# One constant 128x512 product in front of the turns of q, P, x, the sealed rows and the logits, in an attention plus top-2 expert kernel

## The chip, the cores and the metric

The kernel runs on one core of a Trainium2 chip. The core has a matrix engine (TensorE, PE in the profile; its weight loads are shown as PEld), a vector engine (VectorE, DVE), a scalar engine (ScalarE, ACT), GpSimd (POOL) and SyncE (SP), which run their own instruction streams and meet at semaphores. Sixteen DMA engines move data between HBM and the on-chip memory SBUF. TensorE writes only to PSUM, which has eight banks of 128 partitions by 512 float32; the vector and scalar engines read it from there. The metric is the device time of one launch in microseconds (us); a median of several runs is compared.

## The reference

The work is a chunked attention followed by a mixture of experts. There are 4 batches, 8 heads, 768 positions and a head size of 64. Chunks of 32 queries see 16 keys before them, their own 32, 8 after them, and 8 memory keys, 64 in all. The output is 3072 rows of 512 numbers, and each row goes to 2 of 8 experts.

```python
for c in range(nc):                        # 24 chunks of 32 queries
    k_full = np.concatenate([mem_k, k_ctx], axis=2)
    v_full = np.concatenate([mem_v, v_ctx], axis=2)
    scores = scale * np.matmul(q_c, k_full.transpose(0, 1, 3, 2))
    a = np.exp(scores - np.max(scores, axis=-1, keepdims=True))
    out[:, :, c_start:c_end] = np.matmul(a / np.sum(a, -1, keepdims=True), v_full)
x = out.transpose(0, 2, 1, 3).reshape(3072, 512)
noisy_logits = x @ w_gate + np.log1p(np.exp(x @ w_noise)) * noise
top2, top2_w = two largest of noisy_logits, softmax over the two
for e in range(8):                          # F = 1024
    h = np.maximum(x[mask] @ w1[e], 0.0)
    out[mask] += top2_w[mask, k, None] * (h @ w2[e])
```

## The kernel before

**Attention.** Heads are taken in 16 pairs (4 per batch); two pairs form a group, and q, k and v are loaded by group. For every pair q and k are turned on TensorE (`turn`, line 505: 12 transposes of 128x64 each into a PSUM buffer of class Q) and copied to SBUF by ScalarE or VectorE. `scores` (line 529) writes the 24 chunks of one pair to PSUM; VectorE takes the maximum (line 546) and subtracts it (line 562), ScalarE takes the exponential (line 565). The probabilities P are turned by `pt` (line 568: 6 transposes of 128x128 into a PSUM buffer of class G), copied (lines 355 and 357), and multiplied with the values in `pv` (line 581: 6 products with the memory values, line 584, and 24 with the windows, line 587). VectorE divides (line 605) into the rows x. After the second pair of a group `xtp` (line 610) turns x for both pairs, 6 transposes each into a G buffer, and the copies feed `logits` (line 647: 24 products of 16 columns, one G buffer per batch).

**Routing.** Per batch, a chain of small VectorE operations and products (lines 662 to 867: `sel`, `rank`, `place`, `table`, `spare_rank`) finds for each pair of experts the list of its rows; the rows of x go to HBM (line 871). There are 28 pairs of experts with a tile of 128 places each.

**Experts.** Rows are gathered by indirect DMA from POOL (line 907), turned by `xturn` (line 932: 4 transposes per tile), multiplied with w1 (`ups`, line 977, products at line 1013), passed through a relu (line 1023), multiplied with w2 (`downs`, products at line 1054), weighted and added on VectorE, and scattered to the output by POOL (line 1085). For the first two experts half of each tile (the sealed half, `half == 0`) is gathered from the first three batches alone, so that its turns (four of them) and its w1 products lie beside the routing of the last batch.

**Order.** A planner (`Planner`, line 60) simulates the engines with the cost written at each `op` and emits every operation in the order of its start; that order is the order of each engine's instruction stream. An engine takes its instructions in that order, and a waiting one holds up those behind it. The buffers of a class go round: class Q has two PSUM banks, class G two during the attention and six more after it, and a new holder waits until the readers of the former one are done. The q, k, v and weight loads and the gathers are issued by POOL and share its DMA queue; the rows of x are written from SP.

`turn`, `pt`, `xtp` and `xturn` each run their transposes back to back with the moving operand `identb`, the 128x128 identity.

Of the kernel before, what the change touches and what calls it, by code (L numbers as in the profile page):

```python
# [12 lines left out]
F32 = mybir.dt.float32  # L13
# [182 lines left out]
def kernel(  # L196
# [117 lines left out]
    identb = const.tile([128, 128], BF16, name="identb")  # L314
# [36 lines left out]
    V, A, P_, G_ = nc.vector, nc.scalar, nc.tensor, nc.gpsimd  # L351
# [7 lines left out]
    op, buf = pl.op, pl.buf  # L359
    DA = lambda d, a: [("DVE", d), ("ACT", a)]  # L360

    def ident_fn(o):
        make_identity(nc, identb)

# [96 lines left out]
    for g in range(NG):  # L461
        b, gg = divmod(g, 2)
        bq, bk, bv = buf("q"), buf("k"), buf("v")
# [32 lines left out]
    for n in range(NPAIR):  # L496
        g, j = divmod(n, 2)
        b, i = divmod(n, PB)
        bq, bk, bv, lq, lk, lv = groups[g]
# [2 lines left out]
        if i == 0:  # L502
            xrows[b] = buf("xrow")

        def turn(o, src, dst, j=j):
            s = src.t.rearrange("p h (t d) -> p h t d", t=TP)
            for t in range(TP):
                for hh in range(2):
                    P_.transpose(out=dst.t[64 * hh:64 * hh + 64, t * QP:(t + 1) * QP], in_=s[:, j + 2 * hh, t, :], identity=identb)  # L509
# [51 lines left out]
        else:  # L561
            sb = op("sb", ("DVE", 0.98), lambda o, bmx=bmx, bS=bS, bsd=bsd: V.tensor_tensor(  # L562
                out=bsd.t, in0=sv(bS), in1=bmx.t.rearrange("p x (u o) -> p x u o", o=1).to_broadcast([128, 2, BT, CTX]), op=Alu.subtract),
                deps=[mx], alloc=[bsd], use=[bS, bmx], prio=pr - 3, tag="attn")
            ex = op("ex", ("ACT", 0.85), lambda o, bsd=bsd, bP=bP: A.activation(out=bP.t.rearrange("p (x u) h c -> p x (u h) c", x=2), in_=bsd.t, func=Act.Exp, scale=scale), deps=[sb], alloc=[bP], use=[bsd], prio=pr - 2, tag="attn")  # L565
        gP, bPT = buf("G"), buf("PT")

        def pt(o, gP=gP, bP=bP):
            d = gP.t.bitcast(BF16)[:, :BT * 128].rearrange("p (u q) -> p u q", q=128)
            for u in range(BT):  # L570
                P_.transpose(out=d[:, u, :], in_=bP.t[:, u, :, :], identity=identb)
# [36 lines left out]
        gX, bxt = buf("G"), buf("xt")  # L608

        def xtp(o, gX=gX, b=b, i=i):  # L610
            d = gX.t.bitcast(BF16)[:, :BT * 128].rearrange("p (u q) -> p u q", q=128)
            x4 = xrows[b].t.bitcast(BF16)
            for u in range(BT):
                P_.transpose(out=d[:, u, :], in_=x4[:, u, 128 * i:128 * (i + 1)], identity=identb)  # L614
# [11 lines left out]
    for b in range(B):  # L626
# [4 lines left out]
        gL = buf("G")  # L631
# [12 lines left out]
        def lv_(gL=gL):  # L644
            return gL.t[:, :BT * 2 * E].rearrange("p (t e) -> p t e", e=2 * E)

        def logits(o, b=b, lv_=lv_):
            l = lv_()
            for t in range(BT):
                for i in range(PB):  # L650
                    P_.matmul(out=l[:, t, :], lhsT=pairs[b * PB + i]["bxt"].t[:, t, :], rhs=wgn[:, i, :], start=(t == 0 and i == 0), stop=(i == PB - 1), skip_group_check=True)
# [275 lines left out]
    def turn_ops(units, prio, half):  # L927

        gx = buf("G", QM if half == 0 else None)
        m = len(units)  # L930

        def xturn(o):
            d = gx.t.bitcast(BF16)[:, :KP * m * 128].rearrange("p (j k c) -> p j k c", k=KP, j=m)
            for j, (ps, (bx, g)) in enumerate(units):
                s_ = bx.t.bitcast(BF16)
                n = SL if half == 0 and len(ps) == 1 else 128
                for kp in range(KP):
                    P_.transpose(out=d[:, j, kp, :n], in_=s_[:n, kp * 128:(kp + 1) * 128], identity=identb[:n, :n])

        tt = op("tt_a" if half == 0 else "tt", ("PE", 0.27 * m), xturn, deps=[u[1][1] for u in units] + [c_ident], alloc=[gx], use=[u[1][0] for u in units], prio=prio)  # L940
        if half is None:
            i0 = place_of(*units[0][0][0])

            def xev(o):
                copy(o.eng, XS[:, :, i0:i0 + m].rearrange("p k j c -> p j k c"), gx.t.bitcast(BF16)[:, :KP * m * 128].rearrange("p (j k c) -> p j k c", k=KP, j=m))

            w = KP * m * 128
            ev = op("xev", DA(0.2 + w / 1900, 0.2 + w / 1250), xev, deps=[tt], use=[gx], prio=prio)
            for ps, _ in units:
                turned_ev[ps[0], 0] = turned_ev[ps[0], 1] = ev  # L950
            return
        for j, (ps, _) in enumerate(units):
            def xev(o, j=j, ps=ps):
                d = gx.t.bitcast(BF16)[:, 512 * j:512 * j + 512].rearrange("p (k c) -> p k c", k=KP)
                i = place_of(*ps[0])
                if len(ps) == 1:
                    copy(o.eng, XS[:, :, i, SL * half:SL * half + SL], d[:, :, SL * half:SL * half + SL])
                elif half == 0:
                    copy(o.eng, halves_view(XS[:, :, i:i + 2], 0), d.rearrange("p k (x c) -> p k x c", x=2))
                else:  # L960
                    copy(o.eng, XS[:, :, i, SL:], d[:, :, SL:])
                    copy(o.eng, XS[:, :, i + 1, :SL], d[:, :, :SL])

            w = KP * (64 if len(ps) == 1 else 128)
            d_ = 0.4 if half and len(ps) > 1 else 0.2
            ev = op("xev_a" if half == 0 else "xev", ("ACT", 0.2 + w / 1250) if half == 0 else DA(d_ + w / 1900, d_ + w / 1250), xev, deps=[tt], use=[gx], prio=prio)
            for p in ps:
                turned_ev[p, half] = ev
# [256 lines left out]
```

## Time and profile before

| | before |
|---|---|
| median of 3 runs | 334.55 us (332.03 to 334.84) |
| the profiled execution's own time | 331.19 us |
| its span, first to last instruction | 329.6 us |
| TensorE busy | 282.8 us (86%), 3090 products |
| VectorE busy | 161.9 us (49%) |
| ScalarE busy | 141.0 us (43%) |
| GpSimd busy | 127.4 us (39%) |
| mean granted TensorE clock | 0.936 |

The page of the profile shows the span in 40 slices of 8.24 us. The row PEclk is the share of full speed that was granted to TensorE; the trace records it in stretches that are multiples of 3.41 us, each at full or at half speed. A wait's releaser is what ended an engine's idle time; "issue" there means that nothing in the profile was waited for.

### The profile page before, as it was taken

The numbers are of one execution on the slowest core, as the hardware profiler recorded it, in microseconds if no ns is written. First come the engines' busy times: TensorE is split into PE (matmuls) and PEld (weight loads), VectorE is DVE, ScalarE is ACT, GpSimd is POOL, SyncE is SP. The second block draws the span as 40 slices with busy tenths as digits, with TensorE's granted clock in tenths as the row PEclk, the third lists the DMA queues.
The fourth block names the chain that finished last, engine by engine and source line by source line (L and its number), as shares of the span: only waits on it lengthen the run. The fifth ranks groups of instructions, "written<-read, shape, count | busy, mean of one in ns | idle before, by whom it ended". The sixth has DMA issues, their size and how long they took to land.

```text
span 329.6 us, 7497 instructions
## 1 busy us (share of the span) xinstructions
PE 282.8 (86%) x3090; PEld 178.0 (54%) x3090; DVE 161.9 (49%) x404; ACT 141.0 (43%) x265; POOL 127.4 (39%) x148
## 2 busy tenths in 40 slices
PE   1678767587676799799999999999999999999991
PEld 0567655475566567455647645444544744744540
DVE  6877997879889676254253043052042051041050
ACT  1468665656484265741504604604604604505500
POOL 8293353413504915898735221041040051051072
PEclk9999797979785569999999999999999999999997
DMA  9999999999993592939999995395390020021032
GB/s 99 202 157 148 180 148 176 193 133 204 145 166 114 152 153 59 182 98 195 191 215 220 255 196 74 55 207 74 57 203 28 3 113 23 2 111 50 3 121 83
DMA packets 83065, 42.75 MB, mean 130 GB/s; under 512 B 57017, under 2 KB 76474, under 8 KB 83026
## 3 DMA queue, kind: packets, MB, share of 16 engines
q0 software_dynamic: 74672, 38.78, 87.3%
q1 hardware_dynamic: 8066, 3.38, 4.2%
q8 instruction: 25, 0.41, 0.5%
q14 instruction: 14, 0.11, 0.2%
q10 hardware_dynamic: 288, 0.07, 0.1%
HBM read 61.26 MB, written 10.85 MB: 219 GB/s over the span
## 4 chain that ended last, share of the span: by engine, by line
PE 50%; DMA 12%; POOL 12%; issue 11%; DVE 10%; ACT 2%; POOLq 1%; DVEq 0%
PE ps_l L1013 16%; PE ps_l L1054 15%; DMA vg<-in_v_dram 9%; PE ps_g L1054 6%; PE ps_g L1013 5%; POOL xl L907 4%; DMA w2l<-in_moe_w_dram 3%; POOL out_dram L1085 2%; POOL rest L910 2%; POOL vg L479 2%; DVE vg L368 2%; DVE xrow L605 2%; PE ps_o L587 1%; PE ps_g L614 1%; ACT kT L355 1%
## 5 line engine op out<-in xcount | busy, mean ns | idle before, releaser
L1023 ACT ACTIVATE ht<-ps_l 128x384 bf16<-128x384 f32 (+2 forms) x123 | 54.8, 470 | 94.5 <-PE ps_l L1013 93.0
L1054 PEld LDWEIGHTS <-ht 128*128 128x128 bf16 x448 | 43.7, 98 | 52.2 <-DMA w2l<-in_moe_w_dram 0.6
L1013 PE MATMUL ps_l<-XS,w1t 128*128 128x384 bf16 (+4 forms) x416 | 61.0, 302 | 2.8 <-ACT XS L355 2.8
L1013 PEld LDWEIGHTS <-w1t 128*128 128x128 bf16 x544 | 43.9, 99 | 33.4 <-issue 4.3
L1085 POOL DMA_INDIRECT out_dram<-acc,oid x28 | 28.8, 1027 | 70.2 <-DVE acc L1073 66.4
L1054 PE MATMUL ps_l<-w2l,ht 128*128 128x512 bf16 x240 | 53.4, 379 | 0.3 <-DMA w2l<-in_moe_w_dram 0.3
L479 POOL DMA_DIRECT2D vg<-in_v_dram x18 | 23.6, 1314 | 34.7 <-PE ps_o L587 30.6
L1073 DVE SCALAR_TENSOR_TENSOR acc<-ps_l,gates,acc 128x512 f32<-128x512 f32 x17 | 12.8, 751 | 45.6 <-PE ps_l L1054 43.6
L1073 DVE SCALAR_TENSOR_TENSOR acc<-ps_g,gates,acc 128x512 f32<-128x512 f32 x11 | 8.3, 751 | 37.4 <-PE ps_g L1054 37.4
L355 ACT COPY kT<-ps_q 64x768 bf16<-64x768 bf16 x27 | 21.4, 792 | 11.7 <-PE ps_q L509 10.2
L1065 DVE TENSOR_SCALAR acc<-ps_l,gates 128x512 f32<-128x512 f32 x20 | 15.0, 751 | 19.0 <-PE ps_l L1054 18.8
L1054 PE MATMUL ps_g<-w2l,ht 128*128 128x512 bf16 x96 | 21.7, 379 | 0.0
L907 POOL DMA_INDIRECT xl<-x_rows,gid x16 | 16.8, 1049 | 11.6 <-PE ps_l L1054 4.0
L1013 PEld LDWEIGHTS <-w1l 128*128 128x128 bf16 x192 | 17.2, 98 | 7.0
L1013 PE MATMUL ps_l<-XS,w1l 128*128 128x256 bf16 (+3 forms) x152 | 20.5, 289 | 0.0
L509 PE MATMUL ps_q<-identb,qn 128*64 128x128 bf16 x192 | 10.7, 256 | 10.8 <-DMA qn<-in_q_dram 7.3
L1023 ACT ACTIVATE ht<-ps_g 128x384 bf16<-128x384 f32 (+2 forms) x37 | 16.8, 479 | 6.7 <-PE ps_g L1013 5.8
L1013 PE MATMUL ps_g<-XS,w1t 128*128 128x384 bf16 (+4 forms) x128 | 19.6, 300 | 0.0
L919 DVE COPY gates<-xl 64x8 f32<-64x8 f32 (+1 forms) x40 | 11.5, 291 | 14.4 <-DMA xl<-x_rows,gid_b 8.3
L1054 PE MATMUL ps_l<-w2t,ht 128*128 128x512 bf16 x80 | 17.8, 379 | 0.0
L605 DVE TENSOR_TENSOR xrow<-ps_o,rec 128x384 bf16<-128x384 f32 x32 | 16.4, 553 | 0.5
L565 ACT ACTIVATE P<-sd 128x768 bf16<-128x768 f32 x16 | 13.5, 845 | 6.0 <-DVE sd L562 5.8
(170 smaller groups left out, 394.5 us busy)
## 6 DMA issues: line engine op xcount, KB each, us to landing
w1t<-in_moe_w_dram POOLq DMA_DIRECT2D x6, 1024.0 KB
w2l<-in_moe_w_dram POOLq DMA_DIRECT2D x6, 1024.0 KB
vg<-in_v_dram POOLq DMA_DIRECT2D x14, 336.0 KB
qn<-in_q_dram POOLq DMA_DIRECT2D x8, 384.0 KB
kn<-in_k_dram POOLq DMA_DIRECT2D x8, 384.0 KB
x_rows<-xrow SPq DMA_DIRECT2D x3, 792.0 KB, 9.0
w2t<-in_moe_w_dram POOLq DMA_DIRECT2D x2, 1024.0 KB
w1l<-in_moe_w_dram POOLq DMA_DIRECT2D x2, 1024.0 KB
```

The costliest lines, as they stand in the source:

```text
L355: A.copy(dst, src)
L479: G_.dma_start(out=vt.rearrange("p j c h d -> p (j c) h d")[p0 + j:p0 + j + nj, c:c + n, hh, :], in_=bass.AP(v.tensor, v.offset + (hd * S ...
L565: ex = op("ex", ("ACT", 0.85), lambda o, bsd=bsd, bP=bP: A.activation(out=bP.t.rearrange("p (x u) h c -> p x (u h) c", x=2), in_=bsd.t, fu ...
L605: V.tensor_tensor(out=x5[:, x], in0=ov(bO)[:, x, :, :, :D], in1=r5[:, x].to_broadcast([128, UB, 2, D]), op=Alu.mult)
L907: G_.indirect_dma_start(out=bx.t[:n], out_offset=None, in_=src, in_offset=bass.IndirectOffsetOnAxis(ap=ids_[:n, c:c + 1], axis=0), bounds_ ...
L919: V.tensor_copy(gates[rows, cc, :], bx.t[rows, XC:].bitcast(F32))
L1013: P_.matmul(out=dst, lhsT=w1b[e].t[:, kp, f * 128:(f + 1) * 128], rhs=src, start=(kp == 0), stop=(kp == KP - 1), skip_group_check=True)
L1023: A.activation(out=dst, in_=s_, func=Act.Relu)
L1054: P_.matmul(out=gy.t, lhsT=ht.t[:, f, j, :], rhs=w2b[e].t[:, f, :], start=(f == 0), stop=(f == FB - 1))
L1065: V.tensor_scalar(out=ba.t, in0=gy.t, scalar1=gate, scalar2=None, op0=Alu.mult)
L1073: V.scalar_tensor_tensor(out=ba.t, in0=gy.t, scalar=gate, in1=ba.t, op0=Alu.mult, op1=Alu.add)
L1085: G_.indirect_dma_start(out=out_part[nv], out_offset=bass.IndirectOffsetOnAxis(ap=oid[:, c:c + 1], axis=0), in_=ba.t, in_offset=None, boun ...
```

## The change

A helper `run_up(dst)` writes one product into a whole PSUM bank: the stationary operand is the identity `identb`, and the moving operand is the identity four times side by side, 512 columns. It is called as the first thing inside five operations, on the buffer that they are about to write: in `turn` for q alone (16 times; the k turns have none), in `pt` (16), in `xtp` (16), in `logits` (4) and in `xturn` for the sealed half (4), 56 products in all. The products that follow overwrite every column that is read later. The planner's costs are not changed, so the order of every engine's operations is as before; nothing is removed.

```diff
+    def run_up(dst):
+
+        P_.matmul(out=dst, lhsT=identb, rhs=identb.rearrange("p (o c) -> p o c", o=1).to_broadcast([128, 4, 128]), start=True, stop=True, skip_group_check=True)
+
...
-        def turn(o, src, dst, j=j):
+        def turn(o, src, dst, j=j, bq=bq):
             s = src.t.rearrange("p h (t d) -> p h t d", t=TP)
+            if src is bq:
+                run_up(dst.t.bitcast(F32))
...
         def pt(o, gP=gP, bP=bP):
+            run_up(gP.t)
...
         def xtp(o, gX=gX, b=b, i=i):
+            run_up(gX.t)
...
-        def logits(o, b=b, lv_=lv_):
+        def logits(o, b=b, lv_=lv_, gL=gL):
+            run_up(gL.t)
             l = lv_()
...
         def xturn(o):
+            if half == 0:
+                run_up(gx.t)
```

## The prediction, made before the changed kernel was run

> **What bounds the kernel now.** I read the page first, for who is busy where.
>
> ```profile
> span 329.6 us, 7497 instructions
> ...
> DVE  6877997879889676254253043052042051041050
> ...
> PEclk9999797979785569999999999999999999999997
> DMA  9999999999993592939999995395390020021032
> ...
> vg<-in_v_dram POOLq DMA_DIRECT2D x14, 336.0 KB
> ```
>
> A digit is 8.24 us. The DMA engines are full for twelve slices, to about 99 us. VectorE is at 9 in the slice that ends at 82.4. The clock row dips again and again ahead of 120 us and is whole after that. Next I read the chain of waits in order of time (start, us, what).
>
> ```profile
> 57.37 13.30 DMA vg<-in_v_dram
> ...
> 84.20 1.77 issue
> ...
> 103.22 0.81 ACT PT L355
> ...
> 116.20 3.14 PE ps_l L1013 x16
> ...
> 124.19 2.41 PE ps_l L1013 x24
> ...
> 165.15 3.45 PE ps_g L1054 x16
> ```
>
> Up to 70.7 us the chain hangs on the loads of v: 336 KB need about 2.8 us at the 121 GB/s of the window row 65.87 below, yet this one took 13.3 us from issue to landing, so some 10 us of other loads lay ahead of it. From 70.7 to 135.8 us it runs through VectorE, ScalarE and TensorE in turn, and after that TensorE is dense:
>
> ```profile
> 135.75 1.42 PE L1013 MATMUL ps_l<-XS,w1t 128*128 128x384 bf16 x11 [2.08 <-ACT XS L355]
> ```
>
> This 2.08 us is its last idle time of note. So the end comes earlier by what the stretch 70.7 to 135.8 gains, and later by what it loses.
>
> **The clock, read from the work.** Six transposes of P (line 571) are the same work wherever they stand. Their busy time by stretches:
>
> ```profile
> 0.00:28.30 28.30, 2.47 (x18) 1.68 (x18) 1.00 1.46 151
> 38.60:48.00 9.40, 1.51 (x18) 1.02 (x18) 1.00 2.06 161
> 100.00:120.40 20.40, 1.62 (x12) 1.12 (x12) 0.50 0.49 121
> ```
>
> That is 0.50 us for six at full speed and 0.81 at half. The first 28 us show 0.82 beside a clock of 1.00: they ran at half, and the 9s there are a lack of records. Then I laid windows on the grid of 3.41 us on which the clock changes (us, TensorE busy and count, PEld, DVE, ACT, POOL, clock, DMA share, GB/s).
>
> ```profile
> 65.87:69.28 3.41, 3.27 (x58) 2.78 (x58) 2.42 (x4) 0.80 (x1) 1.14 (x2) 0.50 2.73 121
> 82.93:86.35 3.42, 1.38 (x59) 1.07 (x52) 2.89 (x11) 2.48 (x4) 2.62 (x3) 1.00 1.94 155
> 86.35:89.76 3.41, 2.36 (x33) 2.12 (x34) 2.83 (x10) 0.00 (x0) 1.54 (x2) 0.50 2.07 125
> 89.76:93.17 3.41, 3.41 (x72) 2.98 (x72) 2.55 (x5) 2.62 (x5) 0.00 (x0) 0.50 2.01 154
> 93.17:96.59 3.42, 2.64 (x87) 2.39 (x85) 3.07 (x13) 3.18 (x6) 0.00 (x0) 1.00 1.18 209
> 96.59:100.00 3.41, 1.24 (x42) 0.90 (x31) 3.10 (x11) 1.71 (x3) 0.00 (x0) 1.00 0.63 183
> 100.00:103.41 3.41, 1.98 (x43) 1.87 (x43) 3.31 (x10) 1.04 (x2) 0.08 (x1) 0.50 0.31 105
> 103.41:106.83 3.42, 2.99 (x50) 2.46 (x49) 2.83 (x7) 2.15 (x3) 3.21 (x4) 0.50 0.15 40
> 106.83:110.24 3.41, 2.49 (x42) 1.90 (x40) 1.98 (x9) 0.80 (x1) 3.09 (x4) 0.50 0.29 79
> ```
>
> Full windows with TensorE busy 1.38 and 1.24 us are followed by half speed; half-speed windows busy 3.27 and 3.41 us by full speed; those busy 2.36, 1.98, 2.99 and 2.49 us by more half speed. The work itself separates them better: count streamed columns, each weighted by the share of the 128x128 array that it uses.
>
> ```profile
> 67.21 1.46 PE L614 MATMUL ps_g<-identb,xrow 128*128 128x128 bf16 x12
> ...
> 89.13 1.44 PE L614 MATMUL ps_g<-identb,xrow 128*128 128x128 bf16 x12
> 90.36 0.86 PE L584 MATMUL ps_o<-memv,PT 128*128 128x132 bf16 x6
> 91.16 0.83 PE L587 MATMUL ps_o<-vg,PT 128*32 128x128 bf16 x24
> 91.92 0.81 PE L651 MATMUL ps_g<-wgn,xt 128*128 128x16 bf16 x24
> 92.66 0.75 PE L509 MATMUL ps_q<-identb,kn 128*64 128x128 bf16 x12
> ...
> 102.36 0.82 PE L571 MATMUL ps_g<-identb,P 128*128 128x128 bf16 x6
> ...
> 104.07 0.80 PE L614 MATMUL ps_g<-identb,xrow 128*128 128x128 bf16 x6 [0.25 <-ACT PT L355]
> 104.66 0.87 PE L584 MATMUL ps_o<-memv,PT 128*128 128x132 bf16 x6
> 105.46 0.83 PE L587 MATMUL ps_o<-vg,PT 128*32 128x128 bf16 x24
> ```
>
> The window from 89.76 holds about four of the twelve L614 (512), 6x132 = 792, 24x128/4 = 768, 24x16 = 384 and 12x128/2 = 768: 3,220, and the clock came. The one from 103.41 holds two L614 left over (256), 768, 792, 768 and about 160 of the first turn of the next P and small ones: 2,750, and it stayed away. The border lies between. A run-up product adds 512.
>
> **The price of one.** Nothing in the trace before is a run-up, but line 1054 streams 512 columns too: 3.45/16 = 0.22 us at full speed. At half speed line 1013 took 3.14/16 = 0.196 us each against 2.41/24 = 0.100, so I double it: 0.43. Its bounds are nothing, where TensorE would have waited for the data of the next product anyway, and 0.43. It waits for the buffer alone, not for the data.
>
> **To 70.7 us: 0.** By the starts of the five operations in the time order of TensorE thirty run-ups lie here. Cover: the 10 us of loads that stood ahead of the load of v. POOL issues each load of v when `pv` gives up its buffer, so a later `pv` makes a later issue; a delay of a microsecond or two leaves the queue fed. Without that cover they cost up to 30 x 0.43 = 12.9 us, which the full DMA digits exclude.
>
> **70.7 to 84 us: +0.3.** Nine run-ups at full speed are 1.9 us of TensorE beside a VectorE that is the chain; two in front of x turns are waited for by its copies. Bounds 0 and 1.9.
>
> **84 to 93.4 us: +0.8.** The window from 82.93 has no run-up in it and was half empty, so the drop at 86.35 stays. Two x turns and the logits on the chain get one each at half speed: 3 x 0.43 = 1.3. They push the turns out of the window from 86.35 as they add to it, so I expect the clock at 93.17 as before; the 1.3 us pushed beyond it then run at double speed, about -0.5. If the clock comes one window earlier, the 3.65 us from 89.76 to 93.41 halve (-1.8) and the three cost 0.65: -1.2. With +1.3 these are the ends.
>
> **The stall at 84.20: -0.5.** TensorE stood 1.77 us in the middle of `scores` with nothing to wait for. If this is a fetch of instructions at a fixed count, the 39 run-ups ahead of it (thirty and nine) move it into the `pv` before, where the wait for VectorE covers part. Bounds -1.8 and +1.8 (another one moved onto the chain).
>
> **101.4 to 120.5 us: -1.5.** No run-up lies in the window from 96.59, busy for 1.24 us, so the drop at 100 stays. The run-ups in front of P (102.36) and of the second x turn (104.07) lie on the chain at half speed, +0.86; that of the first x turn lies under ScalarE's 0.81 us copy. The window from 103.41 then holds two run-ups more, 2,750 + 1,024 = 3,770 with no idle time left, and the clock comes at 106.83 and not at 120.5 (-0.1 for the rest of that `pv`).
>
> ```profile
> 95.97 0.51 PE L584 MATMUL ps_o<-memv,PT 128*128 128x132 bf16 x6
> 96.40 0.52 PE L587 MATMUL ps_o<-vg,PT 128*32 128x128 bf16 x24
> ...
> 108.72 0.84 PE L584 MATMUL ps_o<-memv,PT 128*128 128x132 bf16 x6
> 109.50 0.83 PE L587 MATMUL ps_o<-vg,PT 128*32 128x128 bf16 x24
> 110.26 1.03 PE L938 MATMUL ps_g<-identb,xl 128*128 128x128 bf16 x8
> ...
> 112.45 0.80 PE L614 MATMUL ps_g<-identb,xrow 128*128 128x128 bf16 x6 [0.20 <-ACT XS L355]
> ```
>
> From there: the `pv` at 108.72, 1.54 us from start to the next operation against twice 0.43 at full speed, -0.66; the sealed turn 1.03 halved plus a run-up, -0.3; the x turn at 112.45, 0.3 less and a run-up, -0.1; sixteen w1 products 3.14 at 0.100 each, -1.5, less the run-up of the second sealed turn ahead of them, and 0.1 kept back since VectorE's choice of the experts runs beside them and would be next, -1.2. The last two run-ups and the faster rank products beside them I set against each other. Sum 0.86 - 0.1 - 0.66 - 0.3 - 0.1 - 1.2 = -1.5; the ends are +2.6 (below) and -2.4, where the first two are hidden too.
>
> After 120.5 us one run-up is left, and the clock is whole: what the chain gained stays.
>
> **Sum.** 0.3 + 0.8 - 0.5 - 1.5 = -0.9 us. The profiled execution's 331.19 becomes 330.3; the median 334.55, which lies 3.4 us above it, becomes 333.6.
>
> **Rivals.**
> *More of the clock.* The grid of 3.41 us lies anew in each execution, and a lucky one brings the clock at 89.76 (-1.2 for +0.8) and moves the stall off the chain (-1.8 for -0.5): 0.3 - 1.2 - 1.8 - 1.5 = -4.2, so 330.3. For it speaks that the runs before spread over 2.8 us; against it that the gaps that cause the drops hold no run-up. Chance 0.28.
>
> *The clock does not come back, slower.* If the columns of transposes (lines 509, 571, 614, 938) did not count, the window from 103.41 would hold about 1,600 + 1,024, fewer than the 2,750 that did not suffice; then the three on the chain ahead of 93 us and six of those from 102 to 120 us (P, two x turns, three sealed turns) cost 0.43 each and nothing is gained: 0.3 + 1.3 + 2.6 = +4.2, so 338.7. It decides from the point where that window falls short. Against it: in the window from 65.87 the x turns alone are 1,536 columns and its k turn is 768, with some 770 of `scores` beside them, and it got the clock; the one from 103.41, with 1,600 columns of other products, did not. [...] Chance 0.14.
>
> *It does not act.* VectorE's order sets the chain from 84 to 120 us as well, and both costs and gains lie beside it: 334.5. Against it, the chain names TensorE for most of 101 to 120 us. Chance 0.16.
>
> The forecast has 0.42.
>
> **Numbers.** About 1% (3.3 us) is what a measurement tells from no change. Below 331.2 lies most of the first rival and an eighth of the forecast: 0.30. Above 337.9 lies nearly all of the second: 0.14. The rest, 0.56, is within. The range from 329.0 to 338.0 takes in the first rival and the forecast with the ends of its terms (333.6 with some 4 us to either side), and leaves out half of the second and the luckiest of the first.
>
> **What would show it.** Right: half speed after 86 and after 100 us, and full speed from about 107 us; the w1 products after 116 us at 0.10 us each; the dense part starting about 1 us earlier than 135.8. Wrong: half speed to 120 us again, or the loads of v waiting behind the run-ups before 70 us.

## The result, and the profile after

Over 20 runs of each kernel the change took 336.57 us (332.74 to 339.91) and the kernel before 333.47 us (332.03 to 335.47). The ratio is 1.0059, with an interval of 1.0035 to 1.0084: the change is slower by 0.6%, about 2.0 us (3.1 us by the two medians), where 0.9 us less was forecast, from a median of 3 runs (334.55) that lay 1.1 us above that of these 20. Medians, here and in all tables, are taken over all runs, while ratios leave out runs more than 1.5% above the fastest of their kernel (5 of the 20 of the change, 5 of the 13 of `after_w2swap` below), so a ratio is not that of the two medians. The time lies inside the range of the prediction, its sign is wrong.

The profiled execution that came with the result took 339.91 us, 3.3 us above its own median. The rows below are therefore mostly those of another profiled execution of the same kernel, called `again`, which took 335.79 us; where the first one says the same, its row stands beside it. Line numbers behind the new helper are 4 to 11 higher than before (1013 is 1024 now, 1054 is 1065), and line 364 is the run-up product; the kernels of the experiments differ by a few lines again.

The page of `again`: span, clock, DMA digits, and the group of the run-ups in front of buffers of class G (busy us, mean ns of one record, idle before).

```profile
span 334.2 us, 7593 instructions
...
PEclk9997999699785979899999999999999999999997
DMA  9999999999993492749999994585581021021032
...
L364 PE MATMUL ps_g<-identb 128*128 128x512 bf16 x38 | 16.4, 432 | 0.5 <-DVE xt L357 0.4
```

The DMA digits are full up to about 100 us, as they were up to 99. The clock row has a dip in the slice that ends at 142, where the row of before showed only 9s from 124 us on.

The chain of waits of `again`, in order of time (start, us, what):

```profile
56.67 13.37 DMA vg<-in_v_dram
...
70.60 0.32 PE ps_g L364
...
71.51 0.23 PE ps_g L364
...
75.16 0.22 PE ps_g L364
...
76.16 0.32 PE ps_q L364
...
76.71 1.12 issue
...
78.30 0.32 PE ps_g L364
...
89.52 0.58 PE ps_g L364
...
90.75 0.43 PE ps_g L364
...
93.23 0.54 PE ps_g L364
...
104.10 0.54 PE ps_g L364
...
105.28 0.43 PE ps_g L364
106.35 0.43 PE ps_g L364
...
121.10 7.85 DMA x_rows<-xrow
...
133.79 3.93 DMA xl<-x_rows,gid_b
...
139.31 6.37 PE ps_l L1024 x48
```

The early part has the same form as before, with run-ups in it. The late part is a different chain. Where the chain of before went through w1 products (the first products of the experts) from 116 us on, this one goes through a write of the last rows (`x_rows`, the 24 KB with the gates of the last batch) and then through a gather, and the first long block of w1 products takes 6.37 us where it took 4.76.

**The clock did what was forecast.** Windows of `again` on its own 3.41 us grid (us, TensorE, PEld, VectorE, ScalarE, POOL busy and count, clock, DMA share, GB/s):

```profile
84.61:88.03 3.42, 2.27 (x72) 1.82 (x72) 3.21 (x12) 1.32 (x2) 2.30 (x3) 1.00 1.19 77
88.03:91.44 3.41, 2.60 (x23) 1.89 (x21) 3.28 (x9) 0.66 (x1) 1.85 (x2) 0.50 2.57 117
91.44:94.86 3.42, 3.42 (x69) 2.72 (x68) 1.46 (x4) 2.08 (x5) 0.00 (x0) 0.50 2.30 148
...
98.27:101.69 3.42, 1.24 (x42) 0.89 (x31) 3.11 (x11) 1.71 (x3) 0.00 (x0) 1.00 0.66 188
101.69:105.10 3.41, 1.99 (x40) 1.61 (x40) 3.31 (x10) 0.84 (x1) 0.00 (x0) 0.50 0.29 100
105.10:108.52 3.42, 3.42 (x44) 2.67 (x44) 2.21 (x5) 1.86 (x3) 2.73 (x3) 0.50 0.15 40
108.52:111.93 3.41, 2.35 (x63) 1.89 (x55) 2.33 (x10) 1.27 (x2) 3.08 (x5) 1.00 0.29 79
...
135.83:139.24 3.41, 0.82 (x10) 0.49 (x8) 1.29 (x6) 2.29 (x8) 2.94 (x5) 1.00 0.79 108
139.24:142.65 3.41, 3.34 (x18) 1.79 (x18) 0.00 (x0) 0.78 (x4) 3.08 (x4) 0.50 1.12 215
```

The dip after 88.03 lasts two windows, as that after 86.35 did. The next one begins at 101.69 behind a window busy for 1.24 us and lasts two windows and not six: the window from 105.10 was full, and full speed came at 108.52 (before: 120.5). What was not foreseen stands in the last two rows: from 135.83 TensorE was busy for 0.82 us only, and the window behind it ran at half speed. (`again` has one more such window, 118.75 to 122.17, behind one that was busy for 2.12 us; the first execution has not.)

The six windows of before are not what that kernel always shows. Counted from this drop to 128 us, the trace of before has six windows at half speed, and so has `tiny` below. Seven other traces with no run-ups in this stretch (`early`, the four `pad` kernels, `w2swap` and `w2late`, all below) have three or four: in `pad40` and `w2swap` full speed came at 107 us, was lost twice more and came back each time. The eleven traces with run-ups of 512 columns here have one to three. So the run-ups do bring more of the clock, but they save two windows on average (2.2 against 4.0) and not four.

**Where the gain went.** TensorE's timeline, first of `again`, then of the first execution (start, us, what, idle before and its releaser):

```profile
118.18 2.62 PE L1024 MATMUL ps_l<-XS,w1t 128*128 128x384 bf16 x16 [1.25 <-ACT XS L355]
...
137.77 0.40 PE L949 MATMUL ps_g<-identb,xl 128*128 128x128 bf16 x4 [1.51 <-DMA xl<-x_rows,gid_b]
139.31 6.37 PE L1024 MATMUL ps_l<-XS,w1t 128*128 128x384 bf16 x48 [1.14 <-ACT XS L355]
```

```profile
121.82 1.69 PE L1024 MATMUL ps_l<-XS,w1t 128*128 128x384 bf16 x16 [0.67 <-ACT XS L355]
...
143.56 6.22 PE L1024 MATMUL ps_l<-XS,w1t 128*128 128x384 bf16 x48 [1.22 <-ACT XS L355]
```

In the first execution the sixteen w1 products took 1.69 us, 0.106 each, as forecast; in `again` most of them fell into the extra window. But TensorE later waited for gathered rows, and paid the dip at 139.24 (143.18 there) in the long block: 6.37 and 6.22 us against 4.76.

POOL's timeline, of before, of `again` and of the first execution, shows what that block waits for:

```profile
115.34 0.98 POOL L887 DMA_DIRECT2D w2t<-in_moe_w_dram  x1
126.25 1.08 POOL L907 DMA_INDIRECT xl<-x_rows,gid_b  x1 [9.92 <-DVE upr L844]
```

```profile
117.64 0.98 POOL L896 DMA_DIRECT2D w2t<-in_moe_w_dram  x1
129.75 1.08 POOL L916 DMA_INDIRECT xl<-x_rows,gid_b  x1 [11.13 <-DVE vs L862]
```

```profile
134.01 1.08 POOL L916 DMA_INDIRECT xl<-x_rows,gid_b  x1 [10.98 <-DMA x_rows<-xrow]
```

POOL issues the sealed gathers, then a 1 MB load of second weights (`w2t`), and then stands idle for 10 to 11 us until the first whole gather may go. The first execution names what it waits for: the write of the gates to `x_rows`, which the gather reads. The VectorE instructions named in the other two only happen to end 0.1 and 0.5 us ahead of the gather and work on other lists. The list that the gather reads was ready by 124.0 us in before and by 126.0 in `again`, 2.3 and 3.8 us earlier (VectorE's timelines):

```profile
123.29 0.68 DVE L760 SCALAR_TENSOR_TENSOR gid_b<-ps_l,tab 64x4 int32<-64x4 f32 x4
```

```profile
125.30 0.68 DVE L769 SCALAR_TENSOR_TENSOR gid_b<-ps_l,tab 64x4 int32<-64x4 f32 x4
```

The chain above puts the write at 7.85 us from 121.10, beside the 1 MB load that was issued at 117.64. The next table is read from such rows of each trace. S is the start of the first sealed gather, W that of the first whole gather, M that of the 48 w1 products, all in us. The first thirteen rows have the loads in their old order; what the kernels are is told in the next section. (The three `w2late` kernels, which have the load elsewhere again, are not in it.)

| kernel | S | S to end of last gates | S to W | W to M | half speed during the 48 products | M to end | S to end |
|---|---|---|---|---|---|---|---|
| before | 103.3 | 16.6 | 22.9 | 9.5 | no | 193.9 | 226.3 |
| change, first execution | 110.0 | 15.3 | 24.0 | 9.6 | yes | 194.7 | 228.3 |
| change, `again` | 105.6 | 15.5 | 24.1 | 9.6 | yes | 194.9 | 228.6 |
| `after_pad40` | 106.8 | 17.0 | 24.4 | 9.4 | no | 193.5 | 227.2 |
| `after_pad72` | 108.5 | 17.9 | 23.5 | 9.1 | no | 195.1 | 227.8 |
| `after_pad88` | 108.6 | 13.8 | 23.2 | 9.4 | no | 194.1 | 226.7 |
| `tiny` | 110.4 | 16.7 | 24.0 | 9.6 | yes | 195.0 | 228.6 |
| `late` | 103.8 | 17.2 | 23.3 | 9.4 | yes | 195.0 | 227.6 |
| `early` | 107.2 | 16.7 | 22.8 | 10.6 | no | 193.3 | 226.7 |
| `pad40` | 106.0 | 14.3 | 23.3 | 9.3 | no | 193.7 | 226.3 |
| `pad64` | 107.0 | 13.7 | 24.0 | 10.0 | yes | 195.1 | 229.1 |
| `pad96` | 105.3 | 15.3 | 23.1 | 8.8 | no | 194.8 | 226.7 |
| `pad128` | 107.1 | 13.5 | 22.6 | 9.4 | yes | 195.2 | 227.2 |
| `w2swap` | 106.4 | 14.9 | 18.4 | 11.7 | no | 193.6 | 223.7 |
| `late_w2swap` | 107.2 | 16.7 | 20.6 | 12.2 | no | 193.4 | 226.2 |
| `late_w2swap_b` | 106.3 | 16.7 | 19.8 | 12.0 | no | 193.3 | 225.0 |
| `after_w2swap` | 112.7 | 16.7 | 19.8 | 12.1 | no | 193.3 | 225.1 |

In the first thirteen rows W does not follow the work ahead of it. The last gates are ready 13.5 to 17.9 us behind S, and W comes 22.6 to 24.4 us behind S all the same: `pad64` has its gates at 13.7 and W at 24.0, `after_pad72` has them at 17.9 and 23.5. What W does keep to is the load, which is issued 12.0 to 12.1 us behind S in all thirteen, 10.6 to 12.3 us ahead of W. So a gain ahead of the last gates or of the list does not pass W.

Against the one trace of before, the two executions of the change are 1.1 to 1.2 us later at W and 2.0 to 2.3 us longer behind S. That is the size of the measured loss, but it does not show that the loss lies there. The three padded versions of the change are as slow as the change or nearly so (1.0033 to 1.0069 below), have no dip in the block of 48, and are only 0.4 to 1.5 us longer behind S than before, while `pad64`, which has no run-ups at all, is 2.8 us longer and has the dip. On average the five traces with all 56 run-ups of 512 columns are 0.6 us longer behind S than the five with none and the old loads (before and its four paddings), and their S lies 2.1 us later; each of these ten is a single execution, and within each group they differ by 1.9 us or more behind S and by 3.8 us or more in S.

### The profile page after: what moved, and what is told of

Read it like the earlier page. It is cut to its first block, busy times and chain, and to the rows that moved or that the text cites. A ratio compares the mean times of both kernels' runs of the same rounds, so it can differ in the third digit from the quotient of the medians.

```text
span 338.3 us, 7593 instructions
## 1 busy us (share of the span) xinstructions
PE 294.7 (87%) x3130; PEld 179.1 (53%) x3146; DVE 160.9 (48%) x404; ACT 142.2 (42%) x265; POOL 127.3 (38%) x148
## 4 chain that ended last, share of the span: by engine, by line
PE 58%; DVE 13%; DMA 12%; issue 8%; POOL 3%; ACT 3%; POOLq 1%; DVEq 0%; ACTq 0%
PE ps_l L1065 17%; PE ps_l L1024 17%; DMA vg<-in_v_dram 8%; PE ps_g L1065 7%; PE ps_g L1024 5%; DMA x_rows<-xrow 2%; DVE xrow L612 2%; POOL out_dram L1096 2%; PE ps_g L364 2%; DVE vg L372 2%; PE ps_o L594 1%; ACT kT L355 1%; PE ps_q L515 1%; PE ps_s L545 1%; DMA xl<-x_rows,gid_b 1%
## 5 line engine op out<-in xcount | busy, mean ns | idle before, releaser
L1034 ACT ACTIVATE ht<-ps_l 128x384 bf16<-128x384 f32 (+2 forms) x123 | 54.9, 467 | 93.9 <-PE ps_l L1024 93.4
L483 POOL DMA_DIRECT2D vg<-in_v_dram x18 | 23.5, 1310 | 39.9 <-PE ps_o L594 37.7
L594 PE MATMUL ps_o<-vg,PT 128*32 128x128 bf16 x384 | 10.3, 253 | 10.9 <-DMA vg<-in_v_dram 7.7
L1034 ACT ACTIVATE ht<-ps_g 128x384 bf16<-128x384 f32 (+2 forms) x37 | 16.7, 474 | 5.8 <-PE ps_g L1024 5.7
L928 DVE COPY gates<-xl 64x8 f32<-64x8 f32 (+1 forms) x40 | 10.5, 273 | 18.1 <-DMA xl<-x_rows,gid_b 13.3
L364 PE MATMUL ps_g<-identb 128*128 128x512 bf16 x38 | 17.0, 447 | 0.9 <-DVE xt L357 0.3
## 6 DMA issues: line engine op xcount, KB each, us to landing
vg<-in_v_dram POOLq DMA_DIRECT2D x14, 336.0 KB, 12.2
kn<-in_k_dram POOLq DMA_DIRECT2D x8, 384.0 KB, 12.1
```

Of the source, the lines that this page charges most:

```text
L364: P_.matmul(out=dst, lhsT=identb, rhs=identb.rearrange("p (o c) -> p o c", o=1).to_broadcast([128, 4, 128]), start=True, stop=True, skip_g ...
L483: G_.dma_start(out=vt.rearrange("p j c h d -> p (j c) h d")[p0 + j:p0 + j + nj, c:c + n, hh, :], in_=bass.AP(v.tensor, v.offset + (hd * S ...
L594: P_.matmul(out=pvw[32 * r:32 * r + 32, u // UB, u % UB, :, :D], lhsT=PT[:, u, 32 * r:32 * r + 32], rhs=vt[:, j, c], start=False, stop=Tru ...
L1034: A.activation(out=dst, in_=s_, func=Act.Relu)
```

## The experiments

All ratios are to the kernel before, measured on the same chip. The expectations name these theories. A: the TensorE time of the run-ups holds up the loads of v early on. B: the added products move the fetches of TensorE's instructions to worse places. C: run-ups after 84 us cost their half-speed time on the chain. D: every added instruction costs at its place, however narrow. E: from the first sealed gather to the first whole one it is POOL's gathers, the load and the gate write, whatever TensorE does. F: any products in front of the first turn cost. These letters are not the marks of the table.

**Narrow run-ups, and parts of the change.** `tiny` keeps all 56 products but makes them 8 columns wide:

```diff
-        P_.matmul(out=dst, lhsT=identb, rhs=identb.rearrange("p (o c) -> p o c", o=1).to_broadcast([128, 4, 128]), start=True, stop=True, skip_group_check=True)
+        P_.matmul(out=dst[:, :8], lhsT=identb, rhs=identb[:, :8], start=True, stop=True, skip_group_check=True)
```

`late` keeps the 17 from the thirteenth pair on (n is the pair), with the logits of the last batch and the sealed turns; `early` keeps the other 39 (`n < 12`). The edit in `pt`, which those in the other four operations follow:

```diff
-            run_up(gP.t)
+            if n >= 12:
+                run_up(gP.t)
```

Expected of `again`:

> The changed kernel once more, for a second profile of it: its first one belongs to an execution of 339.91 us, 3.3 us above its median of 336.57. Theory A (the run-ups ahead of 76 us hold TensorE up, so that the loads of v are issued and land later, and those from 84 to 120 us win clock back): the seventh pv (58.85 us in the kernel before) again starts 2 to 4 us late, and of the lag that stands at 92 us 1 to 2 us are won back by the rank products of the last batch (119.15 before). Theory B (56 more products move the fetches of instructions): the lag appears at one stall with releaser issue of about 3 us near the twelfth pv (82.8 before) and is under 1 us ahead of it. Theory C (the run-ups from 84 us on cost half-speed time on the chain): the lag grows from 84 to 120 us.

Expected of `tiny`:

> All 56 run-ups in their places, but 8 columns wide in place of 512: the same count of instructions and the same waits, with hardly any TensorE time (7 ns at full speed) and no columns for the clock. Theory A: neither cost nor gain, within 0.5 us of the kernel before. Theory B: the full loss, +2 to +4 us. Theory C: as A.

Expected of `late`:

> Run-ups only for the last batch (the q, P and x turns of pairs 12 to 15, the logits of batch 3) and the four sealed turns, 17 of 56 products, nearly all from 74 us on. Theory A: these are the ones that bring the clock back, 1 to 2 us faster than before. Theory B: the fetches move little ahead of 84 us, within 1 us of before. Theory C: they carry the whole loss, +2 to +4 us.

Expected of `early`:

> The other part: run-ups only for batches 0 to 2 (pairs 0 to 11 and their logits), 39 of 56 products, nearly all ahead of 84 us. Theory A: the loss alone, 4 to 5 us slower than before. Theory B: about the whole loss, +2 to +4 us, since 39 more products stand ahead of the stall at 84 us. Theory C: within 0.5 us of before.

| kernel | median, us | ratio | interval |
|---|---|---|---|
| `tiny` | 335.42 | 1.0064 | 1.0028 to 1.0100 |
| `late` | 333.41 | 0.9997 | 0.9961 to 1.0034 |
| `early` | 334.63 | 1.0029 | 0.9994 to 1.0064 |

In `again` the seventh `pv` came 0.5 us late (its second part at 59.31 us against 58.85) and not 2 to 4, and no stall was near 3 us. From 89 to 94 us its lag behind the kernel before grew by 1.3 us, which is what theory C says; from there to the rank products at 120.61 it shrank by 0.2.

`tiny` is the telling one. In its trace (the page's group; TensorE's timeline) the products are 184 ns records, the clock does not come back until 127.6 us, and the sixteen w1 products are as slow as before:

```profile
L364 PE MATMUL ps_g<-identb 128*128 128x8 bf16 x38 | 7.0, 184 | 0.6 <-ACT XS L355 0.2 <-ACT PT L355 0.2
```

```profile
123.28 3.15 PE L1024 MATMUL ps_l<-XS,w1t 128*128 128x384 bf16 x16 [0.71 <-ACT XS L355]
...
144.00 6.41 PE L1024 MATMUL ps_l<-XS,w1t 128*128 128x384 bf16 x48 [1.37 <-ACT XS L355]
```

Yet it loses as much as the change, and S to W is 24.0 us in it too. So the cost of the 512 columns and the clock that they bring come to about nothing at the end; `tiny` lacks both, and cannot tell whether each is nil or one pays for the other. `late` had the clock back at 108.77 and gained nothing (0.9997), where theory A had 1 to 2 us. `early` lost 0.3%, with an interval that takes in no change, where theory A had 4 to 5 us and theory B 2 to 4. (The 7 ns in the expectation of `tiny` is too much for full speed: 0.22 us for 512 columns makes 3 ns for 8, and 7 is what the 0.43 at half speed makes. The records are 184 ns long all the same.)

**Moving the stalls.** The prediction took the stall at 84.20 us for a fetch of instructions at a fixed count. In the traces such stalls ahead of 100 us ("issue", with nothing waited for) lie at places in the count of products that differ by multiples of 128: in before the five of more than 0.2 us, that at 84.20 the last of them, stand ahead of weight loads (one to each product) 484, 612, 740, 996 and 1,380, and in `again` those at 76.71 and 83.84 us lie just 128 apart. That they are fetches of instructions, as the expectations say, is the author's reading; no trace names them so. Narrow products put into TensorE's first wait for data (3 to 7 us) move them and hide in that wait, of which 1.65 us are left with 96; with 40 of them:

```diff
+            if n == 0 and src is bq:
+                for _ in range(40):
+                    P_.matmul(out=dst.t.bitcast(F32)[:32, :8], lhsT=identb[:, :32], rhs=identb[:, :8], start=True, stop=True, skip_group_check=True)
```

Expected of `pad40`, `pad64` and `pad96` (the kernel before with so many):

> The kernel before with 40 such narrow products in front of its first q turn and no run-up anywhere: the fetches are moved by about as many products at 84 us as the change moves them, and no instruction is added on any path. Theory B: the loss without the change, 1 to 3 us slower than before. Theories A and D: no difference, within 0.5 us.

> The same with 64 products, half the distance between two fetches. Theory B: a time of its own that differs from before and from the one with 40, by up to 2 us to either side, since a fetch then falls on the wait of the rank products at 74.9 us. Theories A and D: no difference, within 0.5 us.

> The same with 96 products: a fetch falls on the wait of 0.8 us for VectorE at 88.7 us and not into the scores at 84 us. Theory B: the stall of 1.77 us at 84.2 us is gone from the chain, 1 to 2 us faster than before. Theories A and D: no difference, within 0.5 us.

Expected of `pad128`:

> The kernel before with 128 narrow products in front of its first q turn: one whole distance between two fetches, so that every later fetch falls on the operation on which it falls before. Theory B (the places of the fetches): no difference from before, within 0.7 us, unlike 40 and 64 products (+0.4% and +0.6%). Rival F (any products in front of the first turn cost, wherever the fetches fall): +1 to +2 us, as with 40 and 64.

Expected of `after_pad88`, `after_pad40` and `after_pad72` (the change with so many):

> The changed kernel with 88 more products of 8 columns and 32 weights, all in front of its first q turn, where TensorE waits for the first load of q until 7.3 us. The 40 run-ups ahead of 84 us and these 88 make 128, so that the fetches of instructions (one per 128 products) fall there on the operations on which they fall in the kernel before. Theory B (the moved fetches are the loss): back to the kernel before, within 1 us of it, or faster by what the clock gives. Theory A (the time of the run-ups on TensorE) and theory D (each instruction, however narrow, costs at its place and pushes the loads of v behind the write of the rows x): still 2 to 3 us slower.

> The change with 40 narrow products in front of the first turn of q, in TensorE's first wait for data. Theory B (the loss of the change is where the fetches of its instructions fall): the fetches fall 40 products earlier in the work than in the change, so the time moves away from the change's 336.3 by more than 0.4%, to 334.5 or below where fewer of them fall into scores and pv of the third batch, or to 338 where more do. Theory C with D (the run-ups cost at their own places): 336.3 as the change, within 0.7, whatever the padding. Theory F (any products in front of the first turn cost): 337 to 338.

> The change with 72 narrow products in front of the first turn of q: the 56 run-ups and these make 128, one whole distance between two fetches, so that behind the last run-up the fetches fall where they fall before, and ahead of the first 56 products earlier. Theory B: nearest to before of all kernels that hold the run-ups, 333.5 to 334.8, ratio up to 1.004. Theory C with D: 336.3 as the change, ratio 1.005 to 1.008. Theory F: 337 to 338.

| kernel | median, us | ratio | interval |
|---|---|---|---|
| `pad40` | 334.35 | 1.0040 | 1.0010 to 1.0071 |
| `pad64` | 335.31 | 1.0058 | 1.0022 to 1.0094 |
| `pad96` | 333.48 | 1.0022 | 0.9993 to 1.0050 |
| `pad128` | 334.65 | 1.0015 | 0.9986 to 1.0043 |
| `after_pad40` | 335.25 | 1.0033 | 1.0001 to 1.0064 |
| `after_pad72` | 335.34 | 1.0052 | 1.0016 to 1.0088 |
| `after_pad88` | 336.05 | 1.0069 | 1.0031 to 1.0106 |

The stalls did move. One each, from TensorE's timelines of `pad40`, `pad64` and `pad96`:

```profile
57.47 0.53 PE L512 MATMUL ps_q<-identb,kn 128*64 128x128 bf16 x5 [3.26 <-issue]
```

```profile
34.15 0.29 PE L574 MATMUL ps_g<-identb,P 128*128 128x128 bf16 x2 [1.75 <-issue]
```

```profile
70.07 0.22 PE L542 MATMUL ps_s<-kT,qT 128*32 128x96 bf16 x1 [2.67 <-issue]
```

The same place in the count, the fourth product of one turn of q, cost 0.38 us in the first execution of the change, 1.12 in `again` and 2.98 in `after_w2swap`. The kernels with 40 or 64 products that do nothing and hide in a wait measured 0.4 to 0.6% slower. A whole distance of 128 was cheapest, but its interval overlaps the others. The four kernels that hold all 56 wide run-ups and the old order of loads lie at 1.0033 to 1.0069, the four paddings without a run-up at 1.0015 to 1.0058, so the two ranges overlap. Since one kernel measured twice came out 0.63% apart (`late_w2swap` below), these differences may be the places of the stalls or only the spread of the measurements, and the padding does not show what the change paid for. The gain of 1 to 2 us for `pad96` did not come, nor did the return of `after_pad88` and `after_pad72` to the kernel before.

**Moving the 1 MB load away.** If W waits for the gate write and the write for the load, then W comes sooner without that load. First it was moved behind the second whole gather, in before (`w2late`), in the change and in `late`; then, in the `w2swap` kernels, it took the place of a later load of first weights behind the fourth whole gather, and that load went five gathers further. In the order of emission `o20` is the load of `w2t` and `o12` the later one; the edit of `w2swap`, of which `w2late` has the first three lines and the gather's, with two gathers:

```diff
+            if o.label == "o20":
+                held = o
+                continue
+            if o.label == "o12":
+                held.fn(held)
+                held, full = o, 0
+                continue
             o.fn(o)
+            if o.label == "gather" and held is not None and held.label == "o12":
+                full += 1
+                if full == 5:
+                    held.fn(held)
```

Expected of `w2late`, `after_w2late` and `late_w2late`:

> The kernel before, with the load of the first expert's w2 (issued at 115.3 us) moved behind the second gather of the whole tiles on POOL. Theory E (from the first sealed gather to the first whole gather it is the paced gathers, this load and the 24 KB of gates that crawl beside it, 23 us whatever TensorE does, so what the clock gives there is off the path): the gates land about 2.5 us after their issue at 120, the first whole gather comes at 124 and not at 126.3, and the kernel is 1.5 to 2.5 us faster. Rival (the whole gather waits for the routing on VectorE): no difference, or slower where the load is then late for its products at 142.6.

> The changed kernel with the same load moved. Theory E: it gains at least what the kernel before gains, 2 to 4 us against the change as it is, so about as fast as the unchanged kernel before; the clock that comes earlier now counts. Rival: as the change, 2 to 3 us slower than before.

> Run-ups only for the last batch and the sealed turns, with the load moved. Theory E: 2 to 4 us faster than before, and 0.5 to 1.5 us faster than the kernel before with the load moved, since the routing of the last batch now sets the first whole gather. Rival: no difference from before.

Expected of `w2swap` and `late_w2swap`:

> The kernel before, with the 1 MB load of expert 0's second weights issued by POOL where the load of a later expert's first weights stood, behind the fourth whole gather, and that later load five gathers further on. Theory E (the first whole gather waits for the gate write, and the gate write for the end of this load): the first whole gather comes 17 to 20 us behind the first sealed gather and not 23, and since now no more bytes than before lie ahead of the later gathers, the end comes 1.5 to 3 us earlier, 330.5 to 332. Against E (TensorE's dense part sets the end whenever that gather comes): the gather comes earlier, the stretch from it to the end grows by as much, 333.5.

> The kernel with run-ups from the thirteenth pair on alone, and the same swap of the two loads. If the clock gained from about 107 us on was hidden under the gate write and the load, it counts now: 1 us or more below the kernel with the swap alone, 329.5 to 331. If it is hidden under POOL's gathers and VectorE's choice of the experts as well, the same as the swap alone within 0.4%.

Expected of `late_w2swap_b`, the same kernel measured again, and of `after_w2swap`:

> The same kernel as late_w2swap, timed once more beside another. Theory E with the clock's gain after 101 us now counting: a ratio to before of 0.991 to 0.997, 0.3% or more below the kernel with the swap alone (0.9999). If the first measurement of it was luck: 0.998 to 1.002, as the late run-ups alone (0.9997) and the swap alone.

> The whole change with the swap of the two loads: 56 run-ups. If the late 17 gain 0.6% once the gate write is out of the way, and the early 39 cost what they cost alone (0.3%, up to 0.9% with the interval of that run): a ratio of 0.995 to 1.000, that is 0.6% to 1.1% below the change. If the late ones gain nothing: 1.005 to 1.007 as the change.

| kernel | median, us | ratio | interval |
|---|---|---|---|
| `w2late` | 338.35 | 1.0123 | 1.0082 to 1.0165 |
| `after_w2late` | 338.56 | 1.0110 | 1.0063 to 1.0157 |
| `late_w2late` | 338.03 | 1.0114 | 1.0081 to 1.0148 |
| `w2swap` | 334.32 | 0.9999 | 0.9962 to 1.0037 |
| `late_w2swap` | 332.05 | 0.9937 | 0.9908 to 0.9966 |
| `late_w2swap_b` | 334.07 | 1.0000 | 0.9964 to 1.0036 |
| `after_w2swap` | 334.13 | 0.9984 | 0.9948 to 1.0019 |

`w2late`, POOL's and TensorE's timelines:

```profile
123.50 1.03 POOL L907 DMA_INDIRECT xl<-x_rows,gid_b  x1 [5.34 <-DVE gid_b L760]
```

```profile
137.44 1.03 PE L938 MATMUL ps_g<-identb,xl 128*128 128x128 bf16 x8 [4.66 <-DMA xl<-x_rows,gid]
139.61 6.45 PE L1013 MATMUL ps_l<-XS,w1t 128*128 128x384 bf16 x48 [1.13 <-ACT XS L355]
```

The first whole gather now waits for its list (`gid_b`) and comes 17.4 us behind S, not 22.9. That half of the theory held. But the gather issued next behind the load took 10.24 us to land, TensorE stands for 4.66 us, and the long block pays a dip as well. The three kernels lose 1.1 to 1.2% alike, with and without run-ups.

`w2swap`, POOL's and TensorE's timelines, and after them those of `after_w2swap`:

```profile
124.82 1.03 POOL L907 DMA_INDIRECT xl<-x_rows,gid_b  x1 [6.32 <-DVE gid_b L760]
```

```profile
136.50 4.76 PE L1013 MATMUL ps_l<-XS,w1t 128*128 128x384 bf16 x48 [1.13 <-ACT XS L355]
```

```profile
132.46 1.03 POOL L916 DMA_INDIRECT xl<-x_rows,gid_b  x1 [7.73 <-DVE gid_b L769]
```

```profile
144.53 4.76 PE L1024 MATMUL ps_l<-XS,w1t 128*128 128x384 bf16 x48 [1.19 <-ACT XS L355]
```

With the swap W comes 18.4 to 20.6 us behind S in all four kernels, and now it does follow the work: it starts 0.6 us behind the start of the instructions that write its list, 3.1 to 3.9 us behind the last gates. So it was the load that held W. The last idle time is 1.1 to 1.2 us and the long block takes 4.76 us, with no dip behind 125 us. The whole change is then level with before: 0.9984, an interval that does not touch that of the change alone (1.0035 to 1.0084). But by the medians it is 334.13 against 333.57, 1.0017, and the interval does touch that of `after_pad40`, which has the same 56 run-ups and the old loads. That the loss sits at the load is therefore one measurement's word. The ratio is in the expected range, but the reason given there, that the late run-ups gain 0.6%, did not hold when `late_w2swap` was measured again (1.0000).

The swap did not turn the loss into a gain. The forecast of 1.5 to 3 us for the swap alone failed (0.9999), although its one trace is 2.6 us shorter behind S than that of before. The table shows where most of the earlier W goes: W to M grew from 9.5 to 11.7 to 12.2 us. And the 0.6% that `late_w2swap` showed was not there when the same kernel was measured again. Two measurements of one kernel that lie 0.63% apart, each with an interval of 0.3 to 0.4% to either side, also say how far any single ratio here is to be trusted. No version was found that beats the kernel before.

## Why the prediction was wrong

**The step that failed** is the sentence "After 120.5 us one run-up is left, and the clock is whole: what the chain gained stays." The chain of before named TensorE at 116 to 127 us, but the dense part waits for the first whole gather, some 9.5 us ahead of M, and that gather for a write behind a 1 MB load: in thirteen traces it came 22.6 to 24.4 us behind the first sealed gather, whether the last gates were ready 13.5 or 17.9 us behind it. So what is gained ahead of it did not pass. In `again` the lag behind before was 1.5 us at the rank products (120.61 against 119.15) and 3.5 us at the gather (129.75 against 126.25). The row that should have warned stands in the profile of before: POOL's 9.92 us of idle time at 126.25. The clock was not whole either: in the two executions of the change the block of 48 lost about 1.5 us to half speed. But that dip is in `pad64` and `pad128` too, without run-ups, and not in the three padded versions of the change, so it is not shown to be the run-ups' doing.

**The term of -1.5: right in kind, too large.** From the start of the last `scores` to the rank products it is 17.71 us in before (101.44 to 119.15), 15.39 in the first execution of the change and 17.50 in `again`: -2.3 and -0.2. Over the traces, the eleven with wide run-ups in this stretch take 16.5 us on average, the eight with none 17.0. The execution of before from which the term was worked out had six windows at half speed, where most have three or four. The sixteen w1 products were at 0.106 us each in nine of the eleven.

**The clock, 84 to 120 us: right in `again`.** Half speed behind 88.03 for two windows (three in the first execution), and behind 101.69 for two windows in place of six. The window that brought it back holds two x turns (1,536 columns), 792 and 704 weighted columns of `pv` and one run-up, with a second just ahead of it: 3,544 columns, above the border set between 2,750 and 3,220. The rival "does not come back" had the sign right and the half speed to 120 us wrong. What speaks against its mechanism is the window from 65.87 in the prediction, with some 770 columns that are no transposes: full speed followed it at 69.28, where it did not follow the one from 103.41 with 1,600. The window here does not decide that, since its 2,008 columns that are no transposes could have been enough by themselves. (The prediction's count of the window from 89.76 is a little low: evenly spaced, six of the twelve x turns and ten of the twelve products of the k turn start in it, which makes about 3,350 columns and not 3,220. The border stays between that and 2,750.)

**The price: right.** At half speed the chain has run-ups at 0.43 to 0.58 us (forecast 0.43), at full speed at 0.22 to 0.38 (0.22).

**70.7 to 84 us: mis-sized.** Five run-ups lie on the chain of `again` with 0.32 + 0.23 + 0.22 + 0.32 + 0.32 = 1.41 us, where +0.3 was taken and 1.9 was the end. The cover named, VectorE as the chain, was not there at these places.

**84 to 93.4 us: the mechanism was right.** Three run-ups on the chain, 0.58 + 0.43 + 0.54 = 1.55 us against 1.3, and the clock back at the same distance. The lag of `again` behind before grew from 0.39 us at the products of line 823 (88.67 us in before) to 1.67 at the k turn (92.66), by 1.28 us where +0.8 was taken; the pushed work gave back about 0.3 and not 0.5.

**The stall, -0.5: right place, luck in the sum.** The stall did move into the `pv` before: 1.02 us at 83.84 in `again`, off its chain, and 3.21 us at 86.69 in the first execution, on its chain. But a stall 128 products ahead of it, which the prediction did not count, lies on the chain of `again` with 1.12 us at 76.71. That leaves 0.65 us less than the 1.77, near the -0.5 for another reason. The size belongs to the execution, not to the place.

**To 70.7 us, 0: not refuted.** The load of v on the chain ended at 70.04 in `again` and at 70.67 before; in the first execution the same `pv` began 2.7 us later. Since two executions of one kernel differ by more than that, it stays undecided; `early`, which holds the 30 run-ups of this stretch and 9 more, costs 0.29%, an interval from nothing to 0.64%. Over all traces the term does not look like nothing: the first products of this `pv`, the ninth, start at 72.9 us on average in the nine with run-ups in this stretch (`tiny` among them) and at 70.8 in the eleven with none (69.36 in before). But the profiled executions of the nine lie 1.9 us above their kernels' medians and those of the eleven 0.2 us below, which could be all of it.

**What is settled of the loss and what is not.** Shown: the 512 columns are not needed for the loss (`tiny` loses the same), and a gain ahead of the first whole gather does not pass it while the load stands where it does. With the load swapped the loss was gone, in one measurement. Open: where the 2 us are lost. Behind S (0.6 us on average), ahead of 70 us, and the run-ups on the chain from 70 to 94 us (2.96 us in `again` against 1.6 forecast, before what the pushed work gives back) are all candidates, and none is shown. Open too: why kernels with 40 or 64 idle products measured as slow.

## What to carry to other kernels

Before work is speeded up, follow the wait that ends last behind it to its own engine: here the dense part waited for a gather, and the gather for a write of 24 KB behind a load of 1 MB; that gather came 22.6 to 24.4 us behind the first sealed gather in thirteen traces, with and without the faster products. A long wait on a queue that feeds the dense part is the row to follow first, and the instruction named as its releaser is to be held against what the waiting one reads. One trace of the kernel before is one execution: its six windows at half speed were three or four in most others. And where 40 products that do nothing, hidden in a wait, come out 0.4% slower and one kernel measured twice differs by 0.6%, a gain of that size is to be trusted only with padded controls and repeats beside it.

## What the runs showed of the hardware

A write of 24 KB took 7.85 us (121.10 to 128.95 in `again`) beside a 1 MB load issued 3.5 us ahead of it; in `w2swap`, where no such load was under way, W, which needs that write, came 3.5 us behind the end of the gates, so the write took no longer than that.

The clock fell behind a window that held no single idle time over 1.51 us: in the window from 135.83 of `again` busy time was 0.82 of 3.41 us, with idle times of 1.51 us and, ahead of the block of 48 at 139.31, of 1.14 us; the next window ran at half speed.

TensorE stops at places 128 products apart, or a multiple of that, for 0.2 to 3.3 us in the traces here (ahead of 100 us), where the profile names nothing that was waited for; the page of `again` counts 25 packets with 0.41 MB in a queue of its own for instructions:

```profile
q8 instruction: 25, 0.41, 0.5%
```

That these stalls are fetches is the author's reading, argued from the distance and from their moving with the padding, and no trace shows it; what makes one 0.2 and the next 3.3 us was not found.
